# A diffusion-transformer block on one core: first scale load on ScalarE's queue, weights held until x has landed, early transposes, gate fold by copies

## The chip, the cores and the metric

The kernel runs on one NeuronCore of one Trainium2 chip. TensorE (PE) multiplies matrices, VectorE (DVE), ScalarE (ACT) and GpSimd (POOL) do elementwise work, and SyncE (SP) issues transfers; ScalarE and GpSimd can issue them as well. The transfers of all issuers are carried out by 16 DMA engines. The metric is the device time of one execution in microseconds. Before the change its median over 8 runs is 243.71 us (243.17 to 243.96).

## The reference

`x` is (2, 256, 1152) in bf16, so 512 tokens in all; `c` is (2, 1152). With D = 1152 and two heads of 576:

```python
mod = (_silu(c) @ w_mod).reshape(B, 6, 1, D)
shift_a, scale_a, gate_a, shift_m, scale_m, gate_m = [mod[:, i] for i in range(6)]
h = _layernorm(x, axis=-1) * (1 + scale_a) + shift_a
qkv = (h @ wqkv).reshape(B, N, 3, H, Dh)
attn = _softmax(jnp.einsum('bqhd,bkhd->bhqk', q, k) * Dh ** (-0.5), axis=-1)
a = jnp.einsum('bhqk,bkhd->bqhd', attn, v).reshape(B, N, D) @ wo
x = x + gate_a * a
h2 = _layernorm(x, axis=-1) * (1 + scale_m) + shift_m
m = _gelu(h2 @ w_fc1) @ w_fc2
return x + gate_m * m
```

The six modulation vectors are products of one vector per batch entry with a 1152 by 6912 matrix. The weights, some 50 MB, are read once.

## The kernel before

**Tiles and stages.** The 512 tokens are four tiles of 128 rows; tiles 0 and 1 are batch entry 0, tiles 2 and 3 batch entry 1. D is nine chunks of 128 columns. The stages follow one another on TensorE: k, q, scores, v, attention times v, the output product, the two products of the feed-forward part.

**Order of the work.** The instructions of every engine are executed in the order in which the program lists them (the loop at L819 adds an ordering from each instruction to the next of its engine). Only waits on semaphores decide when. An issued transfer needs one of a ring of eight semaphores, so a transfer issued by SyncE or ScalarE also waits for the one eight places earlier. All weights are issued by SyncE in one fixed order.

**The front.** ScalarE issues `c_sb` (L84) and `touch_x` (L86), a small read of the second batch entry. SyncE issues the four tiles of `x`, in the order 0, 1, 3, 2 (L88), and then, without a wait, the first group of `w_scale_a` (L109: chunks 0 and 1, all nine row blocks), two row blocks of `w_k` (L106), the second group of `w_scale_a`, two row blocks of `w_k`, and so on, then the last three panels of `w_k`, `w_shift_a` and `w_q`.

**Layer norm.** ScalarE sums tiles 0 and 2 (`act_stats`, L208, two passes a tile); VectorE takes tiles 1 and 3 (`stats_piece`, L195). The root of tile 2 is on ScalarE (`act_root`, `root_exp`), that of tile 3 on GpSimd. `norm1` (L235, VectorE) writes the normed tile, first columns 0 to 511, later the rest.

**Scale, transpose, modulate.** `scale_group` (L249) multiplies `w_scale_a` with the vector `sT`, 9 small products for each chunk, into a small accumulator. `scale_add` (L259) adds one. `transpose_x` (L266) turns 128x128 blocks of the normed tiles on TensorE into a bank `pt`. `modulate` multiplies a turned chunk by its scale, on VectorE (L272) or ScalarE (L274), into `hT0`. `k_step(k, ...)` (L282) adds the products of chunk k for six of the nine panels of the k matrix, in 256 columns (one batch entry) or 512 at a time; the other three panels come after (`k_panel`, L311). For chunks 0 to 3 the order is written out by hand (L360 to L397); for later chunks there is a loop (L398), in which the scales of the next two chunks and the transposes of the next chunk are placed ahead of the products of chunk k, or after the first `split` of them.

**The gate of the feed-forward part.** `gate_vector` (L463) forms `gate_m` on VectorE during the first feed-forward product: partial sums over the row blocks (L469, L471), then sums in blocks of 32 columns (L478, L479) into `folded`, 128 partitions of 72 numbers. `gate_vector_finish` (L485) adds the four groups of 32 partitions by two fp32 products with the matrix `fold` (L489), converts them (L491), writes them to DRAM (L493) and reads them back for all partitions (`broadcast_gate`, L458). It is called one panel before the end of the first product. The gate's reader is L810, the first step after each group of the second product (L804).

Of the kernel before, what the change touches and what calls it, by code (L numbers as in the profile page):

```python
# [19 lines left out]
def kernel(  # L20
# [11 lines left out]
    nc = tc.nc  # L32
    B, N, D = x.shape
# [3 lines left out]
    P = 128  # L37
    T = B * N
    NT = T // P
    TPB = N // P  # L40
    KD = D // P
    KF = F // P
# [20 lines left out]
    def aux_tile(shape, name, dt=FP32):  # L63
        return psum.tile(shape, dt, name=name, tag="aux", bufs=2)


    x_v = x.rearrange("b (p l) d -> p b l d", l=TPB)
    out_v = out.rearrange("b (p l) d -> p b l d", l=TPB)
    c_v = c.rearrange("b (k p) -> (b k) p", p=P)
    wqkv_v = wqkv.rearrange("(k p) n -> p k n", p=P)  # L70
# [11 lines left out]
    x_sb = act.tile([P, NT, D], BF16, name="x_sb", tag="x_sb")  # L82
# [2 lines left out]
    touch_x = act.tile([P, 32], BF16, name="touch_x")  # L85
    nc.scalar.dma_start(touch_x[:], x_v[:, 1, 0, 0:32])  # L86
    for t in (0, 1, 3, 2):
        nc.sync.dma_start(x_sb[:, t, :], x_v[:, t // TPB, t % TPB, :])  # L88

    zeros = const.tile([P, T], BF16, name="zeros")  # L90
    nc.vector.memset(zeros[:], 0.0)
    ident = const.tile([P, P], BF16, name="ident")
# [7 lines left out]
    SGROUPS = [(0, 2), (2, 4), (4, 6), (6, 8), (8, 9)]  # L100
    KM1 = 6
    w_scale_a = wide_tile("w_scale_a")
    w_k = wide_tile("w_k")

    def load_k(k0, k1, c0, c1):
        nc.sync.dma_start(w_k[:, k0:k1, c0:c1], wqkv_v[:, k0:k1, D + c0:D + c1])  # L106

    for k0, k1 in SGROUPS:
        nc.sync.dma_start(  # L109
            w_scale_a[:, :, k0 * P:k1 * P],  # L110
            wmod_v[:, :, S_SCALE_A * D + k0 * P:S_SCALE_A * D + k1 * P],
        )
        for a, z in [(0, 1), (1, 2)] if k0 == 0 else [(k0, k1)]:
            load_k(a, z, 0, KM1 * P)
    load_k(0, KD, KM1 * P, D)

    first_load = {}
# [12 lines left out]
    for (j0, j1), rows in zip(SHG, QROWS):  # L130
# [16 lines left out]
    hT0 = aT  # L147
# [8 lines left out]
        act_func_set_id=LN_EXP_TABLES, name=nc.get_next_instruction_name(),  # L156
        engine=mybir.EngineType.Activation,
    ))
    neg_half = const.tile([P, B], FP32, name="neg_half")
    nc.gpsimd.memset(neg_half[:], -0.5)  # L160
    early = small.tile([P, 1], FP32, name="early", tag="early", bufs=1)
# [6 lines left out]
    pwarm = acc_tile([P, T], "pwarm")  # L168
# [65 lines left out]
    def norm1(t, c0, c1):  # L234
        nc.vector.tensor_scalar(  # L235
            xns[t][:, c0:c1], x_sb[:, t, c0:c1], mv1[:, t, 0:1], rstd1[:, t:t + 1],
            op0=ALU.subtract, op1=ALU.mult,
        )


    scale_a = act.tile([P, KD, B], FP32, name="scale_a")

    def scale_group(k0, k1, tile_of=aux_tile):
        pm = tile_of([P, k1 - k0, B], "pm")
        for j in range(k0, k1):
            if j == 0:
                nc.tensor.matmul(pm[:, 0, :], ones_row[:], ones_row[:, 0:B], start=True, stop=False)
            for k in range(KD):
                nc.tensor.matmul(  # L249
                    pm[:, j - k0, :], w_scale_a[:, k, j * P:(j + 1) * P], sT[:, k, 0:B],  # L250
                    start=(k == 0 and j > 0), stop=(k == KD - 1),
                )
        return pm
# [7 lines left out]
    def transpose_x(ks, ts, pt=None, j0=0):  # L261
        if pt is None:
            pt = aux_tile([P, len(ks), len(ts) * P], "pt", BF16)
        for j, t in enumerate(ts, j0):
            for i, k in enumerate(ks):
                nc.tensor.transpose(pt[:, i, j * P:(j + 1) * P], xns[t][:, k * P:(k + 1) * P], ident[:])  # L266
        return pt

    def modulate(pt, i, k, b, j0, eng):
        dst, src, sc = hT0[:, k, b * N:(b + 1) * N], pt[:, i, j0:j0 + N], scale_a[:, k, b:b + 1]  # L270
        if eng == "d":
            nc.vector.tensor_scalar_mul(dst, src, sc)  # L272
        else:
            nc.scalar.mul(dst, src, sc)  # L274

    pk = [None] * KD

    def k_step(k, c0=0, c1=T, m0=0, m1=KM1):
        for m in range(m0, m1):
            if k == 0 and c0 == 0:  # L280
                pk[m] = acc_tile([P, T], "pk")
            nc.tensor.matmul(  # L282
                pk[m][:, c0:c1], w_k[:, k, m * P:(m + 1) * P], hT0[:, k, c0:c1],
                start=(k == 0 and c0 == 0), stop=(k == KD - 1), skip_group_check=True,
            )
# [30 lines left out]
    CUT = 4 * P  # L316
# [5 lines left out]

    def fill(n):
        for _ in range(n):
            nc.tensor.matmul(pwarm[:], zeros[:, 0:P], zeros[:], start=True, stop=True)

    def pool_eps(t):
        nc.gpsimd.tensor_scalar_add(mv1[:, t, 1:2], mv1[:, t, 1:2], LN_EPS)
# [30 lines left out]
    pool_rsqrt(3, 4)  # L359
    norm1(1, 0, CUT)  # L360
    norm1(0, 0, CUT)
    pt_a = transpose_x([0, 1], BT[0])
    act_mean_eps(2)
    act_root(2)
    root_exp(2, 3)
# [3 lines left out]
    nc.vector.tensor_copy(scale_a[:, 0:1, :], pm0[:])  # L369
    scale_add(pm1, 1, 2)  # L370
    modulate(pt_a, 1, 1, 0, 0, "d")
    norm1(2, 0, CUT)
    pt_c = aux_tile([P, 2, N], "pt", BF16)
    transpose_x([0, 1], [3], pt_c, 1)
    fill(1)
    k_step(0, 0, N)
    k_step(1, 0, N, 0, 2)
    transpose_x([0, 1], [2], pt_c, 0)
    k_step(1, 0, N, 2)
    modulate(pt_c, 0, 0, 1, 0, "d")  # L380
    modulate(pt_c, 1, 1, 1, 0, "a")
    norm1(0, CUT, D)
    norm1(1, CUT, D)
    k_step(0, N, T)
    pm = scale_group(2, 4)
    pt_b = transpose_x([2, 3], BT[0])
    scale_add(pm, 2, 4)
    modulate(pt_b, 0, 2, 0, 0, "d")
    modulate(pt_b, 1, 3, 0, 0, "a")
    norm1(2, CUT, D)  # L390
    k_step(1, N, T)
    pt_d = transpose_x([2, 3], BT[1])
    modulate(pt_d, 0, 2, 1, 0, "d")
    modulate(pt_d, 1, 3, 1, 0, "a")
    norm1(3, CUT, D)
    k_step(2, 0, N)
    k_step(2, N, T)  # L397
    for k in range(3, KD):  # L398
        split = 2 if k == 5 else 0
        k_step(k, 0, T, 0, split)  # L400
        if k in (3, 5, 7):
            k1 = min(k + 3, KD)
            scale_add(scale_group(k + 1, k1), k + 1, k1)
        if k < KD - 1:
            both(transpose_x([k + 1], range(NT)), k + 1)
        k_step(k, 0, T, split)
    for m in range(KM1):
        k_evac(m)

# [38 lines left out]

    s32 = const.tile([P, KD, B], FP32, name="s32")
    nc.vector.tensor_copy(s32[:], sT[:, :, 0:B])  # L450
    fold = const.tile([P, 32], FP32, name="fold")
    nc.vector.tensor_reduce(fold[:], ident[:].rearrange("p (q a) -> p a q", a=32), axis=AX.X, op=ALU.add)
    gates_dram = tc.dram_tile([2, B, D], BF16, name="gates_dram")

    def broadcast_gate(g):
# [7 lines left out]
    def gate_vector(g, wg):  # L463
        part = act.tile([P, B, D], FP32, name="part", tag="x_sb")
        folded = small.tile([P, B, D // 32], FP32, name="folded", tag="folded", bufs=1)
        for k in range(KD):
            for b in range(B):
                if k == 0:
                    nc.vector.tensor_scalar_mul(part[:, b, :], wg[:, k, :], s32[:, k, b:b + 1])  # L469
                else:  # L470
                    nc.vector.scalar_tensor_tensor(  # L471
                        part[:, b, :], wg[:, k, :], s32[:, k, b:b + 1], part[:, b, :],
                        op0=ALU.mult, op1=ALU.add,
                    )
        for b in range(B):
            for c in range(0, D, PW):
                blocks = work.tile([P, PW // 32, 32], FP32, name="tmp", tag="tmp", bufs=3)
                nc.vector.transpose(blocks[:].rearrange("p j r -> p (j r)"), part[:, b, c:c + PW])  # L478
                nc.vector.tensor_reduce(  # L479
                    folded[:, b, c // 32:(c + PW) // 32], blocks[:], axis=AX.X, op=ALU.add  # L480
                )

        return lambda: gate_vector_finish(g, folded)

    def gate_vector_finish(g, folded):  # L485
        rows = D // 32
        pg = aux_tile([rows, B, 32], "pg")
        for b in range(B):
            nc.tensor.matmul(pg[:, b, :], folded[:, b, :], fold[:], start=True, stop=True)  # L489
        nat = work.tile([rows, B, 32], BF16, name="nat_v", tag="nat_v", bufs=1)  # L490
        nc.vector.tensor_copy(nat[:], pg[:])  # L491
        for b in range(B):
            nc.gpsimd.dma_start(gates_dram[g, b, :].rearrange("(j r) -> j r", r=32), nat[:, b, :])  # L493
        return broadcast_gate(g)

    def gate_natural(g, wg):
# [279 lines left out]
    for m in range(MSPLIT, KF):  # L776
        pacc = acc_tile([P, T], "pacc")
        for k in range(KD):
            f1_mm(pacc[:], m, k, 0, T, k == 0)
        nc.scalar.activation(gT[:, m, :], pacc[:], ACT.Gelu_apprx_tanh)  # L780
        if m == 22:
            gate_m_finish = gate_vector(1, w_gate_m)
        if m == KF - 2:
            gate_m = gate_m_finish()
        if m == MSPLIT:
            load_f2(0)
        if m > MSPLIT and m % KD == KD - 1:
            load_f2(m // KD)
# [70 lines left out]
```

## Time and profile before

| what | value |
|---|---|
| median of 8 runs | 243.71 us |
| profiled execution: its time, its span | 243.5 us, 241.7 us |
| TensorE busy | 236.2 us, 98% of the span |
| VectorE, ScalarE, GpSimd busy | 91.4, 60.0, 28.2 us |
| moved from HBM | 50.15 MB, 212 GB/s over the span |
| granted TensorE clock | 1.00 |

The span is the time from the first to the last instruction of the profiled execution; what lies around it is 1.8 us. The page gives for each engine its busy time; the chain of work that ended last, which follows back from the last instruction what released each step; groups of instructions with their mean duration; and issues of transfers with the time from issue to landing. L numbers are lines of the kernel before. `PEld` is TensorE's loading of weights, `SPq` and `ACTq` are the issuing sides of SyncE and ScalarE. A line of the timeline has start, duration, engine, line, operation, output and input, and in brackets the idle time before it with what ended it.

### The profile page before, as it was taken

Reading aid. Unit: us, or ns where it says so; the run is one execution under the profiler, and the core shown is the slowest. Engines: PE = TensorE matmul, PEld = TensorE weight load, DVE = VectorE, ACT = ScalarE, POOL = GpSimd, SP = SyncE. Lnnn points to the kernel's source line nnn. Section 1 sums busy time; section 2 is a strip of 40 time slices with the busy share of each in tenths; the row PEclk is TensorE's granted clock in tenths of the full one; section 3 lists DMA queues with packets and bytes.
Section 4 is the critical chain, followed back from the end, with each engine's and each line's share of the span. In section 5 each row is a group of like instructions: output and inputs, shape, how many; then the busy total and the mean of one; then the engine's idle time right before and its main releaser. Section 6 shows DMA issues by size and latency. Waiting matters only on the chain.

```text
span 241.7 us, 3979 instructions
## 1 busy us (share of the span) xinstructions
PE 236.2 (98%) x1688; PEld 144.9 (60%) x1698; DVE 91.4 (38%) x193; ACT 60.0 (25%) x121; POOL 28.2 (12%) x47
## 2 busy tenths in 40 slices
PE   8899999999999999999999999999999999999994
PEld 5685444465567566888844444444665666655674
DVE  4742442319325678831002999950010000000001
ACT  6633322307215032671422333322000000000000
POOL 2300000001400324100000000001121111111111
PEclk9999999999999999999999999999999999999999
DMA  6999999996499993739999999999200000000000
GB/s 205 325 315 313 378 367 392 390 391 231 111 322 395 389 289 78 195 59 356 392 390 392 340 327 287 277 327 282 97 17 16 20 16 16 19 18 17 25 26 16
DMA packets 48926, 53.30 MB, mean 221 GB/s; under 512 B 9732, under 2 KB 36620, under 8 KB 48908
## 3 DMA queue, kind: packets, MB, share of 16 engines
q1 hardware_dynamic: 41312, 50.14, 62.2%
q10 hardware_dynamic: 7083, 1.72, 4.7%
q0 software_dynamic: 512, 1.19, 1.8%
q8 instruction: 13, 0.21, 0.4%
q14 instruction: 6, 0.04, 0.1%
HBM read 50.15 MB, written 1.19 MB: 212 GB/s over the span
## 4 chain that ended last, share of the span: by engine, by line
PE 94%; DMA 2%; ACT 1%; SPq 1%; issue 0%; DVE 0%; DVEq 0%; ACTq 0%
PE pacc L804 29%; PE pacc L748 29%; PE pacc L695 7%; PE pacc L601 7%; PE pq L523 7%; PE pk L282 5%; PE pk L311 2%; DMA x_sb<-in_x_dram 2%; PE pa L642 2%; PE ps_s L558 2%; PE pn L418 2%; ACT sink L208 1%; PE pt L266 1%; PE pm L249 1%; SPq L88 1%; PE pg L500 0%
## 5 line engine op out<-in xcount | busy, mean ns | idle before, releaser
L748 PE MATMUL pacc<-hT,w_f 128*128 128x256 bf16 (+1 forms) x427 | 70.3, 325 | 0.3
L804 PE MATMUL pacc<-w_f,gT 128*128 128x384 bf16 (+2 forms) x468 | 70.5, 314 | 0.0
L804 PEld LDWEIGHTS <-gT 128*128 128x128 bf16 x468 | 44.4, 98 | 26.2
L748 PEld LDWEIGHTS <-w_f 128*128 128x128 bf16 x432 | 42.2, 98 | 27.6
L810 DVE TENSOR_TENSOR tmp<-pacc,gate 128x384 f32<-128x384 f32 (+2 forms) x13 | 6.9, 527 | 65.6 <-PE pacc L804 56.9
L780 ACT ACTIVATE gT<-pacc 128x512 bf16<-128x512 f32 x24 | 14.3, 597 | 32.7 <-PE pacc L748 32.7
L471 DVE SCALAR_TENSOR_TENSOR part<-w_gate_m,s,part 128x1152 f32<-128x1152 bf16 x16 | 21.4, 1416 | 0.0
L812 POOL TENSOR_TENSOR o_sb<-tmp,x 128x384 bf16<-128x384 f32 (+1 forms) x12 | 11.7, 972 | 54.0 <-DVE tmp L810 54.0
L695 PE MATMUL pacc<-w_o,big 128*128 128x384 bf16 x108 | 17.9, 326 | 0.0
L523 PE MATMUL pq<-hT,w_q 128*128 128x512 bf16 x79 | 17.7, 379 | 0.1
L601 PE MATMUL pacc<-w_v,hT 128*128 128x384 bf16 x108 | 17.7, 326 | 0.0
L601 PEld LDWEIGHTS <-hT 128*128 128x128 bf16 x108 | 10.5, 98 | 7.1 <-issue 0.3
L695 PEld LDWEIGHTS <-big 128*128 128x128 bf16 x108 | 10.4, 98 | 7.2 <-issue 0.4
L523 PEld LDWEIGHTS <-w_q 128*128 128x128 bf16 x81 | 7.9, 98 | 9.4
L282 PE MATMUL pk<-big,w_k 128*128 128x256 bf16 (+1 forms) x70 | 13.1, 324 | 0.1
L701 POOL TENSOR_TENSOR x<-tmp,x_sb 128x384 f32<-128x384 f32 x8 | 7.3, 912 | 26.8 <-DMA w_scale_m<-in_w_mod_dram 14.9
L469 DVE TENSOR_SCALAR part<-w_gate_m,s 128x1152 f32<-128x1152 bf16 x2 | 1.6, 818 | 22.2 <-DMA w_gate_m<-in_w_mod_dram 22.2
L493 POOL DMA_DIRECT2D gates_dram<-nat_v x2 | 1.1, 534 | 67.7 <-DVE nat_v L491 67.7
L282 PEld LDWEIGHTS <-w_k 128*128 128x128 bf16 x72 | 6.7, 98 | 3.7 <-issue 0.3
L769 ACT ACTIVATE gT<-pacc 128x512 bf16<-128x512 f32 x12 | 6.5, 598 | 9.1 <-PE pacc L748 9.1
L175 PE MATMUL pwarm<-zeros 128*128 128x256 f32 x18 | 7.1, 565 | 1.2 <-DVE eps_t L95 1.2
L514 POOL DMA_DIRECT2D gates_dram<-nat x4 | 2.3, 584 | 49.8 <-DVE nat L511 48.8
(102 smaller groups left out, 164.8 us busy)
## 6 DMA issues: line engine op xcount, KB each, us to landing
w_f<-in_w_fc_dram SPq DMA_DIRECT2D x12, 864.0 KB, 14.3
w_f<-in_w_fc_dram SPq DMA_DIRECT2D x3, 1728.0 KB, 10.0
w_f<-in_w_fc_dram SPq DMA_DIRECT2D x2, 2592.0 KB, 17.2
w_gate_a<-in_w_mod_dram SPq DMA_DIRECT2D x3, 864.0 KB, 13.0
w_v<-in_wqkv_dram SPq DMA_DIRECT2D x3, 864.0 KB, 13.8
w_o<-in_wo_dram SPq DMA_DIRECT2D x3, 864.0 KB, 13.9
w_shift_m<-in_w_mod_dram SPq DMA_DIRECT2D x3, 864.0 KB, 8.8
w_scale_m<-in_w_mod_dram SPq DMA_DIRECT2D x3, 864.0 KB, 15.4
```

What stands on the lines that cost most here:

```text
L175: nc.tensor.matmul(dst[:, 0:T // 2], zeros32[:, 0:P], zeros32, start=True, stop=True)
L282: nc.tensor.matmul(pk[m][:, c0:c1], w_k[:, k, m * P:(m + 1) * P], hT0[:, k, c0:c1], start=(k == 0 and c0 == 0), stop=(k == KD - 1), skip_g ...
L471: nc.vector.scalar_tensor_tensor(part[:, b, :], wg[:, k, :], s32[:, k, b:b + 1], part[:, b, :], op0=ALU.mult, op1=ALU.add,)
L523: nc.tensor.matmul(pq[m][:], w_q[:, k, m * P:(m + 1) * P], hT[:, k, :], start=(k == 0), stop=(k == KD - 1), skip_group_check=True,)
L601: nc.tensor.matmul(pacc[:], hT[:, k, t * P:(t + 1) * P], w_v[:, k, pnl * PW:(pnl + 1) * PW], start=(k == 0), stop=(k == KD - 1),)
L695: nc.tensor.matmul(pacc[:], aT[:, k, t * P:(t + 1) * P], w_o[:, k, c0:c1], start=(k == 0), stop=(k == KD - 1),)
L701: (nc.gpsimd if pool_add else nc.vector).tensor_tensor(x1[:, t, c0:c1], tmp[:], x_sb[:, t, c0:c1], op=ALU.add)
L748: nc.tensor.matmul(dst, w_f1[m // KD][:, k, ml * P:(ml + 1) * P], hT[:, k, c0:c1], start=start, stop=(k == KD - 1), **kw,)
L780: nc.scalar.activation(gT[:, m, :], pacc[:], ACT.Gelu_apprx_tanh)
L804: nc.tensor.matmul(pacc[:], gT[:, kk, t * P:(t + 1) * P], w_f2[j][:, r, c0 - n * PW:c0 - n * PW + cw], start=(kk == 0), stop=(kk == KF - 1),)
L810: nc.vector.tensor_tensor(tmp[:], pacc[:], gate_m[:, b, c0:c0 + cw], op=ALU.mult)
L812: (nc.vector if last else nc.gpsimd).tensor_tensor(o_sb[:], tmp[:], x1[:, t, c0:c0 + cw], op=ALU.add)
```

## The change

1. **Loads.** The first group of `w_scale_a` (chunks 0 and 1) is issued by ScalarE, after the load of its function tables. SyncE's first load of `w_k` waits until the last tile of `x` (tile 2) has landed; all later loads of SyncE stand behind it.
2. **Transposes.** Chunks 0 to 3 of tiles 0 and 1 are turned in one go into `pt_a`, chunks 0 to 3 of tile 3 into `pt_c`; of tile 2 chunks 0 and 1 at the old place, 2 and 3 where `pt_b` was. The banks `pt_b` and `pt_d` are gone.
3. **Scale of chunks 2 and 3.** Its accumulator is a piece of `pt_a`, where chunk 0 of tile 0 stood.
4. **Modulation.** Chunks 2 and 3 of batch entry 0 are VectorE's, those of entry 1 ScalarE's. Of chunk 0 of entry 1, tile 3's half is ScalarE's and tile 2's half VectorE's.
5. **Norm.** Tile 2's first 512 columns are normed in two pieces of 256. Tile 3's rest is normed earlier.
6. **The loop.** At chunks 3 and 5 three of the six products stand ahead of the next scale group (before: none at 3, two at 5). At chunks 4 and 6 the products are done in two halves of 256 columns. The filling product `fill` has 256 columns instead of 512.
7. **Gate fold.** The products with `fold` are replaced: GpSimd copies the four groups of 32 partitions of `folded` side by side, VectorE sums, transposes and converts them, and two transfers write them to DRAM. All is done at panel 22, without a second part at panel 34.

```diff
     for t in (0, 1, 3, 2):
-        nc.sync.dma_start(x_sb[:, t, :], x_v[:, t // TPB, t % TPB, :])
+        last_x = nc.sync.dma_start(x_sb[:, t, :], x_v[:, t // TPB, t % TPB, :])
...
     def load_k(k0, k1, c0, c1):
-        nc.sync.dma_start(w_k[:, k0:k1, c0:c1], wqkv_v[:, k0:k1, D + c0:D + c1])
-
-    for k0, k1 in SGROUPS:
-        nc.sync.dma_start(
+        return nc.sync.dma_start(w_k[:, k0:k1, c0:c1], wqkv_v[:, k0:k1, D + c0:D + c1])
+
+    def load_scale(eng, k0, k1):
+        eng.dma_start(
             w_scale_a[:, :, k0 * P:k1 * P],
             wmod_v[:, :, S_SCALE_A * D + k0 * P:S_SCALE_A * D + k1 * P],
         )
+
+    for k0, k1 in SGROUPS:
+        if k0:
+            load_scale(nc.sync, k0, k1)
         for a, z in [(0, 1), (1, 2)] if k0 == 0 else [(k0, k1)]:
-            load_k(a, z, 0, KM1 * P)
+            load = load_k(a, z, 0, KM1 * P)
+            if a == 0:
+                tc.add_manual_dep(load.ins, last_x.ins.name, WAIT_FOR, reason="x first")
...
         engine=mybir.EngineType.Activation,
     ))
+    load_scale(nc.scalar, *SGROUPS[0])
...
-    def scale_group(k0, k1, tile_of=aux_tile):
-        pm = tile_of([P, k1 - k0, B], "pm")
+    def scale_group(k0, k1, tile_of=aux_tile, pm=None):
+        if pm is None:
+            pm = tile_of([P, k1 - k0, B], "pm")
...
-    def modulate(pt, i, k, b, j0, eng):
-        dst, src, sc = hT0[:, k, b * N:(b + 1) * N], pt[:, i, j0:j0 + N], scale_a[:, k, b:b + 1]
+    def modulate(pt, i, k, b, j0, eng, c0=0, c1=N):
+        dst, src, sc = hT0[:, k, b * N + c0:b * N + c1], pt[:, i, j0 + c0:j0 + c1], scale_a[:, k, b:b + 1]
...
-            nc.tensor.matmul(pwarm[:], zeros[:, 0:P], zeros[:], start=True, stop=True)
+            nc.tensor.matmul(pwarm[:, 0:N], zeros[:, 0:P], zeros[:, 0:N], start=True, stop=True)
...
-    pt_a = transpose_x([0, 1], BT[0])
+    pt_a = transpose_x([0, 1, 2, 3], BT[0])
...
-    norm1(2, 0, CUT)
-    pt_c = aux_tile([P, 2, N], "pt", BF16)
-    transpose_x([0, 1], [3], pt_c, 1)
+    norm1(2, 0, N)
+    norm1(2, N, CUT)
+    pt_c = aux_tile([P, 4, N], "pt", BF16)
+    transpose_x([0, 1, 2, 3], [3], pt_c, 1)
     fill(1)
     k_step(0, 0, N)
     k_step(1, 0, N, 0, 2)
+    modulate(pt_c, 0, 0, 1, 0, "a", P, N)
     transpose_x([0, 1], [2], pt_c, 0)
     k_step(1, 0, N, 2)
-    modulate(pt_c, 0, 0, 1, 0, "d")
+    modulate(pt_c, 0, 0, 1, 0, "d", 0, P)
     modulate(pt_c, 1, 1, 1, 0, "a")
     norm1(0, CUT, D)
     norm1(1, CUT, D)
     k_step(0, N, T)
-    pm = scale_group(2, 4)
-    pt_b = transpose_x([2, 3], BT[0])
+    pm = pt_a[:, 0, 0:4 * B].bitcast(FP32).rearrange("p (j b) -> p j b", b=B)
+    scale_group(2, 4, pm=pm)
+    for i in (2, 3):
+        nc.tensor.transpose(pt_c[:, i, 0:P], xns[2][:, i * P:(i + 1) * P], ident[:])
     scale_add(pm, 2, 4)
-    modulate(pt_b, 0, 2, 0, 0, "d")
-    modulate(pt_b, 1, 3, 0, 0, "a")
+    for b, e in enumerate("da"):
+        for i in (2, 3):
+            modulate((pt_a, pt_c)[b], i, i, b, 0, e)
     norm1(2, CUT, D)
+    norm1(3, CUT, D)
     k_step(1, N, T)
-    pt_d = transpose_x([2, 3], BT[1])
-    modulate(pt_d, 0, 2, 1, 0, "d")
-    modulate(pt_d, 1, 3, 1, 0, "a")
-    norm1(3, CUT, D)
     k_step(2, 0, N)
     k_step(2, N, T)
     for k in range(3, KD):
-        split = 2 if k == 5 else 0
+        split = 3 if k in (3, 5) else 0
...
-        k_step(k, 0, T, split)
+        for c0, c1 in ((0, N), (N, T)) if k in (4, 6) else ((0, T),):
+            k_step(k, c0, c1, split)
...
-        pg = aux_tile([rows, B, 32], "pg")
-        for b in range(B):
-            nc.tensor.matmul(pg[:, b, :], folded[:, b, :], fold[:], start=True, stop=True)
-        nat = work.tile([rows, B, 32], BF16, name="nat_v", tag="nat_v", bufs=1)
-        nc.vector.tensor_copy(nat[:], pg[:])
-        for b in range(B):
-            nc.gpsimd.dma_start(gates_dram[g, b, :].rearrange("(j r) -> j r", r=32), nat[:, b, :])
+        quads = small.tile([32, P // 32, B * rows], FP32, name="quads", tag="quads", bufs=1)
+        for a in range(P // 32):
+            nc.gpsimd.dma_start(quads[:, a, :], folded[32 * a:32 * (a + 1), :, :].rearrange("p b j -> p (b j)"))
+        total = small.tile([32, 96], FP32, name="total", tag="total", bufs=1)
+        nc.vector.memset(total[:], 0.0)
+        nc.vector.tensor_reduce(
+            total[:, 0:B * rows], quads[:].rearrange("p a c -> p c a"), axis=AX.X, op=ALU.add,
+        )
+        turned = small.tile([32, 96], FP32, name="turned", tag="turned", bufs=1)
+        nc.vector.transpose(turned[:], total[:])
+        nat = small.tile([32, 96], BF16, name="nat_v", tag="nat_v", bufs=1)
+        nc.vector.tensor_copy(nat[:], turned[:])
+        flat = gates_dram[g, :, :].rearrange("b (j r) -> (b j) r", r=32)
+        nc.gpsimd.dma_start(
+            flat[0:64, :].rearrange("(q c) r -> c q r", q=2), nat[:, 0:64].rearrange("c (q r) -> c q r", q=2),
+        )
+        nc.gpsimd.dma_start(flat[64:B * rows, :], nat[0:B * rows - 64, 64:96])
         return broadcast_gate(g)
...
         if m == 22:
-            gate_m_finish = gate_vector(1, w_gate_m)
-        if m == KF - 2:
-            gate_m = gate_m_finish()
+            gate_m = gate_vector(1, w_gate_m)
```

More of the change, by code (lines that the diff above doesn't have):

```diff
@@ L267, in transpose_x @@
         return pt
-    def modulate(pt, i, k, b, j0, eng):
-        dst, src, sc = hT0[:, k, b * N:(b + 1) * N], pt[:, i, j0:j0 + N], scale_a[:, k, b:b + 1]
+    def modulate(pt, i, k, b, j0, eng, c0=0, c1=N):
+        dst, src, sc = hT0[:, k, b * N + c0:b * N + c1], pt[:, i, j0 + c0:j0 + c1], scale_a[:, k, b:b + 1]
         if eng == "d":
-            nc.vector.tensor_scalar_mul(dst, src, sc)
-        else:
-            nc.scalar.mul(dst, src, sc)
+            return nc.vector.tensor_scalar_mul(dst, src, sc)
+        return nc.scalar.mul(dst, src, sc)
     pk = [None] * KD
@@ L450 @@
     nc.vector.tensor_copy(s32[:], sT[:, :, 0:B])
-    fold = const.tile([P, 32], FP32, name="fold")
-    nc.vector.tensor_reduce(fold[:], ident[:].rearrange("p (q a) -> p a q", a=32), axis=AX.X, op=ALU.add)
     gates_dram = tc.dram_tile([2, B, D], BF16, name="gates_dram")
@@ L481, in gate_vector @@
                 )
-        return lambda: gate_vector_finish(g, folded)
-    def gate_vector_finish(g, folded):
         rows = D // 32
-        pg = aux_tile([rows, B, 32], "pg")
-        for b in range(B):
-            nc.tensor.matmul(pg[:, b, :], folded[:, b, :], fold[:], start=True, stop=True)
-        nat = work.tile([rows, B, 32], BF16, name="nat_v", tag="nat_v", bufs=1)
-        nc.vector.tensor_copy(nat[:], pg[:])
-        for b in range(B):
-            nc.gpsimd.dma_start(gates_dram[g, b, :].rearrange("(j r) -> j r", r=32), nat[:, b, :])
+        quads = small.tile([32, P // 32, B * rows], FP32, name="quads", tag="quads", bufs=1)
[15 more added lines that the diff above has]
+        nc.gpsimd.dma_start(flat[64:B * rows, :], nat[0:B * rows - 64, 64:96])
         return broadcast_gate(g)
```

## The prediction

> **What bounds the kernel now.** I read the page's shares first, then the chain that ended last, then the front of the run.
>
> ```profile
> PE 94%; DMA 2%; ACT 1%; SPq 1%; issue 0%; DVE 0%; DVEq 0%; ACTq 0%
> ```
>
> TensorE sets the end. Only what it executes after it starts in earnest, and what makes it start late, can move the time. The chain in order of time:
>
> ```profile
> 2.10 5.38 DMA x_sb<-in_x_dram
> ...
> 7.50 1.36 ACT sink L208 x2
> ...
> 8.88 1.36 ACT sink L208 x2
> ...
> 10.64 0.21 ACT rstd L340
> ...
> 10.94 0.42 DVE xn L235
> ...
> 11.41 0.28 PE pt L266 x2
> ...
> 12.95 0.43 PE pm L249 x18
> 13.38 0.25 PE pt L266 x4
> 13.63 0.66 PE pk L282 x6
> 14.28 0.22 PE pt L266 x4
> ...
> 166.04 0.26 PE pg L489 x4
> ```
>
> (Start, length, what.) The last x tile, issued at 2.10 us, lands at 7.48. ScalarE's statistics, the root and VectorE's norm follow, and tile 2's transposes start at 11.41. From there TensorE is solid, so a later x tile is paid almost one for one. The two pt rows and the pg row are removable work.
>
> The DMA issues from 2.5 to 3.0 us (size, us from issue to landing), SyncE and ScalarE in time order at the front, and the busy time and GB/s while the first scale load moves:
>
> ```profile
> w_scale_a<-in_w_mod_dram SPq DMA_DIRECT2D x1, 576.0 KB, 6.8
> x_sb<-in_x_dram SPq DMA_DIRECT2D x1, 288.0 KB, 5.4
> ```
>
> ```profile
> 1.15 1.38 SPq L88 DMA_DIRECT2D x_sb<-in_x_dram  x3
> ...
> 1.38 0.36 ACTq L86 DMA_DIRECT2D touch_x<-in_x_dram  x1
> ...
> 1.77 1.28 ACT L155 ACT_TABLE_LOAD   x1 [1.77 <-issue]
> ...
> 2.57 0.43 SPq L109 DMA_DIRECT2D w_scale_a<-in_w_mod_dram  x1
> ```
>
> ```profile
> 6.50:7.00 0.50, 0.50 (x3) 0.41 (x2) 0.50 (x3) 0.48 (x2) 0.23 (x1) 1.00 1.08 331
> ```
>
> The scale load is issued after all x and lands at 2.57 + 6.8 = 9.4, when its products start (9.46). Its 590 KB occupy the engines for 590/331 = 1.8 us. Whatever it is put ahead of waits that long. The last view is ScalarE in the softmax stage:
>
> ```profile
> 57.59 0.49 ACT L581 ACTIVATE soft<-ps_s,negmax 128x256 f32<-128x256 f32 x1
> 57.84 1.34 ACTq L552 DMA_TRANSPOSE soft<-soft  x1
> ...
> 58.04 0.49 ACT L581 ACTIVATE soft<-ps_s,negmax 128x256 f32<-128x256 f32 x1
> ```
>
> All eight L581 instructions stand before the transpose in the program, yet it is issued while one runs and others are still to come. ScalarE's sequencer issues a DMA ahead of its unfinished computation.
>
> **What the Trainium skill says.** "DMA: Bandwidth & Descriptors", Issuing engines are not separate DMA queues: DMAs issued by ScalarE and SyncE run on the same 16 engines and interleave. The same page, Queues, rings and completion order: an engine takes the queues in turns, by packets of some descriptors, and the two issuers have a ring each. The trace agrees on sharing: from 3.50 to 4.25 us the DMA view has ScalarE's queue (q10, touch_x's small packets) beside SyncE's x. It does not show the turns.
>
> ```profile
> q10 hardware_dynamic: 144, 0.01, 12.9%
> ```
>
> "ScalarE: Activation LUTs", What ACT_TABLE_LOAD costs: about 1283 ns for the load, and it is an instruction of the engine; here 1.28 us. The page does not say that the issuing side is held meanwhile.
>
> **The change part by part.**
>
> *Work removed from TensorE.* Chunks 2-3 of tiles 0 and 1 are now transposed at 8.4 us, while TensorE waits for scales, and those of tile 3 ahead of the first k step. At 13.38 and 14.28 stood 0.25 + 0.22 = 0.47 us for eight transposes; two stay, 2 x 0.055 = 0.11: -0.36. The fold product goes: -0.26. Together -0.62 us. The shorter filler lies in a wait: 0.
>
> *Fold by copies.* VectorE is done with the blocks at 160.8 us. Four copies at 0.55 us of issue (L493's rate), some 2.6 to landing, about 1.2 of small VectorE work, two stores (1.1 + 3.6) and the broadcast (1.1 + 4.0) end near 176, against 175.2 now. Its reader L810 then has six accumulators of 5.86 us each from 168.3 before TensorE stops, at about 203. That cover hides it: 0.
>
> *Norm in two, ScalarE for a half.* Tile 2's transposes need only the first 256 columns, 0.28 instead of 0.42 us. But they write the bank from which ScalarE reads tile 3's half of chunk 0, and the built program makes them wait for that 0.37 us piece, behind the root at 10.84: about 11.2. Gain 0.1. If ScalarE's piece is slower, nothing. Chunks 2-3: after the scale products VectorE needs 0.16 + 0.35 before k step 2 starts, TensorE has 0.11 + 0.66 in between; ScalarE's 0.47 pieces have one half step more. Cover 0.2 us: 0. Scale 2-3 in the old bank waits only for a reader finished at 10.2: 0; the trace has no such shared bank, so up to 0.1 lost, nothing to gain.
>
> *Later scale groups.* Groups 4-5 are needed half a step (0.65) later than now; their landing (15.54, issue 8.14 + 7.4) leaves 0.1 to 0.3 now. This holds the k stage together if weights come late. Half-width k steps stream the same columns: 12 in 1.31 us, as 6 wide ones: 0.
>
> *First scale load on ScalarE.* It follows touch_x and the table load. If issue runs ahead of the table load, as at 57.84, it goes out at about 1.8, whereas the last x goes out at 2.06 to 2.10 (a fourth issue of 0.43 after 0.73). It then lies ahead of the x tile that sets the chain. Bounds: x not delayed (7.48) or the full 1.8 (9.3). I take 1.6, near the upper end, since touch_x too moved in the order of issue, before the later x tiles: 9.1. Behind this x tile stands more: VectorE's L215 waits for tile 2's sum (x + 1.4 = 10.5), and behind it in VectorE's order are tile 3's norm, hT0's first chunk and the scale copies, for which TensorE waits.
>
> *k loads after x.* SyncE's whole queue stops until x has landed. Then w_k 0, w_k 1 and scale 2-3 are issued 0.5 us apart. Without backlog the first x took 2.9 us to landing (0.73 to 3.63); w_k 0 is smaller: x + 2.3 to 2.8. w_k 1 adds 0.6, scale 2-3 590 KB at 310 GB/s, 1.9: it lands at x + 5.0 to 5.5. Now it lands at 4.66 + 7.8 = 12.46 with x at 7.48, so x + 5.0. With x on time this costs 0 to 0.5, since the removed backlog pays for the wait.
>
> *Sum.* The scale 2-3 products start at x + 5.47 now (12.95). After: computation path x + 5.37, load path x + 5.0 to 5.5, so about x + 5.4. With x at 9.1: 14.5, +1.5; less 0.62: +0.9 us. Later weight loads shift with TensorE and keep their margin (the k panel: landed about 24.2, needed 25.7). The span becomes 242.6, this execution 244.4; the median of the runs stands 0.2 above the profiled 243.5, so **244.6**.
>
> **Rivals.**
>
> *Issue behind x.* The table load holds the issue to 3.05, or the engines serve x first: x stays at 7.48. Then -0.1 + 0.1 - 0.62: about -0.6, **243.1**. This ends on the other side; it decides where the scale load delays x by less than 0.1 to 0.2 us, since below that the gain passes 0.5. For it: the table load stands between. Against: 57.84.
>
> *Turns.* The engines alternate, as the skill says, and x loses only part: 0.4 to 0.9. Then +0.6 - 0.62 = 0: **243.8**. For it: the skill; against: touch_x came in one piece.
>
> *x alone is quicker.* Nothing competes, and x lands by 6.8. ScalarE is free from 7.23, so its path gains 0.25, and the loads start 0.6 earlier: -0.4 - 0.62 = -1.0: **242.7**. Against: the x loads already lead their queue, and DMA's share is near 1 there either way.
>
> **How the numbers follow.** Scale ahead of x 0.51; turns 0.22; behind x 0.17; x quicker 0.10. The likeliest gives 244.6, own range 244.1 to 245.3 (x 8.6 to 9.5, load path to +0.5). All cases: 242.8 to 245.4. A measurement can tell about 0.2%, 0.49 us, from no change. Faster: x quicker 0.10 and most of behind x (0.14) = 0.24; same: most of turns, a rest of behind x and of the first = 0.22; slower 0.54.
>
> **What would show it.** The issue of the scale load at 1.8, not 3.05; landing of tile 2 of x at 9 or later, ScalarE idle before L208's second pair by over 1.5 us; SyncE's w_k issue right after that; scale 2-3 products at 14.5 with DMA as releaser at the front. No pg product near 166 and six fewer transposes in the chain. I am wrong if x lands by 7.6, or if TensorE waits for loads after 15 us.

## The result

| | before | changed |
|---|---|---|
| median of the runs | 243.61 us (243.08 to 245.02) | 247.09 us (245.63 to 248.38) |
| profiled execution: time, span | 243.5, 241.7 us | 245.63, 243.8 us |
| last tile of x landed | 7.47 us | 8.79 us |
| scale 2-3 landed | 12.5 us | 15.36 us |
| products of scale 2-3 start | 12.95 us | 15.41 us |
| q stage starts | 32.55 us | 35.01 us |
| second feed-forward product starts | 168.34 us | 170.44 us |

The changed kernel is slower: ratio 1.0134, 95% interval [1.0117, 1.0152], or +3.3 us. The forecast had the sign and the place, and 2.5 us too little. The profiled execution is the quickest of its kernel's runs, so its trace explains 2.1 us of the loss; what the others add is found further down. (247.09 is the median of eleven times; the list of runs has a twelfth, 246.08, with which it would be 246.95.)

The shares of the chain that ended last, in the page of the changed kernel, and then that chain in order of time (start, length, what):

```profile
PE 85%; DMA 7%; SPq 5%; issue 1%; DVE 0%; DVEq 0%
```

```profile
2.10 6.70 DMA x_sb<-in_x_dram
8.79 0.02 issue
8.81 0.33 SPq L106
...
9.66 0.43 SPq L109
...
21.42 10.70 DMA w_shift_a<-in_w_mod_dram
32.11 0.04 issue
32.16 0.81 PE pn L428 x36
...
35.01 5.18 PE pq L538 x24
...
167.26 3.19 PE pacc L763 x14
170.44 70.30 PE pacc L817 x468
```

Before, TensorE held 94% of this chain and transfers 2%. Now the chain runs from the late x tile into SyncE's queue, then into a weight load, and reaches TensorE only at 32 us. The end is quiet: no fold product stands between the two feed-forward products, and the 468 products of the second take 70.30 us in both kernels.

The timeline of the changed kernel at the front (start, duration, engine and line, what, and in brackets the idle time before it with what ended it):

```profile
1.78 1.28 ACT L161 ACT_TABLE_LOAD   x1 [1.78 <-issue]
1.81 0.41 ACTq L109 DMA_DIRECT2D w_scale_a<-in_w_mod_dram  x1
...
8.82 1.25 ACT L215 ACTIVATE sink<-x_sb 128x1152 f32<-128x1152 bf16 x1 [1.44 <-DMA x_sb<-in_x_dram]
...
15.41 0.60 PE L257 MATMUL pt<-sT,w_scale_a 128*128 128x2 bf16 x18 [1.20 <-DMA w_scale_a<-in_w_mod_dram]
```

ScalarE's issuing side sent the scale load at 1.81 us, while the table load that stands ahead of it in the program was running, and 0.3 us before SyncE's last x tile went out at 2.10. ScalarE then waits for x, and TensorE waits at 15.41 for scale 2-3. Two loads stop TensorE, as the list of its waits over the first 35 us says (total, times, longest):

```profile
PE pt L257 <- DMA w_scale_a<-in_w_mod_dram: 1.2, 1, 1.2
...
PEld L428 <- DMA w_shift_a<-in_w_mod_dram: 0.6, 1, 0.6
```

What the DMA engines did meanwhile is in the busy times by stretch. The last two columns are their busy share and GB/s. First the kernel before, then the changed one:

```profile
8.00:11.00 3.00, 2.39 (x35) 1.64 (x34) 1.77 (x9) 2.69 (x6) 1.30 (x4) 1.00 1.12 325
11.00:14.00 3.00, 2.90 (x42) 2.30 (x41) 1.89 (x7) 0.47 (x1) 0.00 (x0) 1.00 1.13 319
```

```profile
8.00:11.00 3.00, 1.75 (x29) 1.21 (x28) 2.48 (x8) 2.15 (x3) 1.33 (x4) 1.00 0.48 137
11.00:14.00 3.00, 2.79 (x34) 2.07 (x30) 2.38 (x9) 1.77 (x6) 0.00 (x0) 1.00 0.96 237
```

The engines run dry. From 8 to 14 us they move 3 x (137 + 237) = 1,120 KB instead of 3 x (325 + 319) = 1,930 KB. At 322 GB/s the missing 810 KB are 2.5 us of transfer, about the 2.46 us by which the products of scale 2-3 are late. The match is rough: between 5 and 8 us another 150 KB are missing (250 against 300 GB/s), and a landing also depends on how evenly the 16 engines finish, as is shown further down.

### The profile page after: what moved, and what is told of

The parts are those of the page before. It is cut to its first block, busy times and chain, and to the rows that moved or that the text cites. A ratio compares the mean times of both kernels' runs of the same rounds, so it can differ in the third digit from the quotient of the medians.

```text
span 243.8 us, 4006 instructions
## 1 busy us (share of the span) xinstructions
PE 236.2 (97%) x1695; PEld 146.1 (60%) x1706; DVE 92.4 (38%) x196; ACT 60.1 (25%) x122; POOL 30.3 (12%) x51
## 4 chain that ended last, share of the span: by engine, by line
PE 85%; DMA 7%; SPq 5%; issue 1%; DVE 0%; DVEq 0%
PE pacc L817 29%; PE pacc L763 29%; PE pacc L710 7%; PE pacc L616 7%; PE pq L538 7%; DMA w_shift_a<-in_w_mod_dram 4%; SPq L106 4%; DMA x_sb<-in_x_dram 3%; PE pa L657 2%; PE ps_s L573 2%; PE pn L428 2%; PE pk L318 1%; SPq L109 1%; SPq L88 1%; PE pg L515 0%
## 5 line engine op out<-in xcount | busy, mean ns | idle before, releaser
L616 PEld LDWEIGHTS <-hT 128*128 128x128 bf16 x108 | 10.5, 98 | 7.1 <-issue 0.3
L494 POOL DMA_DIRECT2D quads<-folded x4 | 2.0, 508 | 62.2 <-DVE total L496 62.2
L289 PEld LDWEIGHTS <-w_k 128*128 128x128 bf16 x84 | 7.9, 98 | 2.5 <-issue 0.2
## 6 DMA issues: line engine op xcount, KB each, us to landing
w_scale_m<-in_w_mod_dram SPq DMA_DIRECT2D x3, 864.0 KB, 14.5
```

What stands on the lines that cost most here:

```text
L289: nc.tensor.matmul(pk[m][:, c0:c1], w_k[:, k, m * P:(m + 1) * P], hT0[:, k, c0:c1], start=(k == 0 and c0 == 0), stop=(k == KD - 1), skip_g ...
L616: nc.tensor.matmul(pacc[:], hT[:, k, t * P:(t + 1) * P], w_v[:, k, pnl * PW:(pnl + 1) * PW], start=(k == 0), stop=(k == KD - 1),)
```

## The experiments

Two causes were in question: the scale load that overtakes x ("late x"), and SyncE's queue, which stops until x has landed ("the hold"). The forecast's theory was that late x costs nearly all and the hold at most 0.5 us; the rival that the hold alone, by emptying the DMA engines, costs as much or more.

**e1: the change with its loads as before.**

```diff
-        if k0:
-            load_scale(nc.sync, k0, k1)
+        load_scale(nc.sync, k0, k1)
...
-            if a == 0:
-                tc.add_manual_dep(load.ins, last_x.ins.name, WAIT_FOR, reason="x first")
...
-    load_scale(nc.scalar, *SGROUPS[0])
```

> The changed kernel, but with all loads where they were before: first scale load by SyncE behind x, no hold of the k loads. Theory L (the loads alone cost; the rest removes 0.36 + 0.26 us of TensorE work and 0 to 0.1 of waiting): x lands at 7.5, scale 2-3 at 12.5, the time is 243.0, 0.5 to 0.7 us under the kernel before. Rival R (part of the loss is in the rest: shared bank, later scale groups, halves of k steps): 244 or more, with a wait of TensorE on VectorE or ScalarE between 11 and 25 us.

Measured: 242.92 us, 0.9974 [0.9962, 0.9986], as the theory had it. x landed at 7.49, scale 2-3 at 12.45, as before. All of the loss is in the loads; the rest of the change gains 0.3% or 0.6 us (interval 0.3 to 0.9), the size of the work removed.

**e2: the loads alone.** The kernel before, with part 1 of the change (loads) and nothing else.

```diff
-    for k0, k1 in SGROUPS:
-        nc.sync.dma_start(
...
+    def load_scale(eng, k0, k1):
+        eng.dma_start(
...
+    for k0, k1 in SGROUPS:
+        if k0:
+            load_scale(nc.sync, k0, k1)
...
+            if a == 0:
+                tc.add_manual_dep(load.ins, last_x.ins.name, WAIT_FOR, reason="x first")
...
+    load_scale(nc.scalar, *SGROUPS[0])
```

> The kernel before with only the change of the loads: first scale load by ScalarE behind the table load, k loads held until x has landed. Theory L: the whole loss and none of the gain, so 0.6 us above the changed kernel, about 247.7; with none of its scale groups needed later, up to 0.5 more. Rival R: clearly under the changed kernel, 246 or less.

Measured: 246.87 us, 1.0132 [1.0116, 1.0148]. x landed at 8.19 and scale 2-3 at 14.98, 6.8 us behind it. The loads alone cost as much as the whole change, 247.09, and not the 0.6 us more that was expected (247.7). So the 0.6 us that e1 gains is not to be seen, within these intervals, while TensorE waits for loads. That fits work taken out ahead of a wait, which only lengthens the wait; it is not shown alone, since in e2's profile x and scale 2-3 also land 0.6 and 0.4 us sooner than in the changed kernel.

**e3: late x alone, and e4: the hold alone.** e3 takes the wait out of the changed kernel; e4 keeps the wait and gives the first scale load back to SyncE, behind x.

```diff
-            if a == 0:
-                tc.add_manual_dep(load.ins, last_x.ins.name, WAIT_FOR, reason="x first")
```

```diff
-        if k0:
-            load_scale(nc.sync, k0, k1)
+        load_scale(nc.sync, k0, k1)
...
-    load_scale(nc.scalar, *SGROUPS[0])
```

> The changed kernel without the hold: k loads go out behind x at once, the first scale load stays with ScalarE. If the place of the scale load ahead of the last x tiles is the cause: x lands at 8.5 to 9.4 as in the changed kernel, scale 2-3 at about 12.5 to 13, the time is set by x + 5.4 and the removed work, 244.0 to 244.8. If the hold is the whole cause: 243.0. If the hold is without effect: 247.

> The changed kernel with the hold, but the first scale load by SyncE behind x as before. x lands at 7.5, scale 2-3 at x + 6.6 (as measured in the changed kernel, not x + 5.0 to 5.5 as I had it) = 14.1, its products 1.1 later than before; less 0.6 of removed work: 244.0 to 245.0. If the restart of the stream costs nothing (x + 5.2): 243.2. If the hold is the whole cause: 247.

Measured: e3 245.40 us, 1.0075 [1.0052, 1.0098]; e4 245.42 us, 1.0076 [1.0051, 1.0101]. Against e1 each cause costs 2.5 us by the medians of four runs, and each is there without the other. Both medians lie over what was expected (244.0 to 244.8, and 244.0 to 245.0). Two of the four runs of each have a lower clock, of which more below; at full clock the costs are 1.8 and 1.7 us. So the rival was right about the hold: alone it costs as much as late x. In e3 the last x tile lands at 2.10 + 7.62 = 9.72 us. The scale load itself comes later there too (11.18 us, 9.41 before), but the chain still runs through x. In e4 x lands in time (7.44), and yet scale 2-3 comes 7.15 us behind it; the chain of waits of e4 and its timeline:

```profile
2.10 5.34 DMA x_sb<-in_x_dram
...
8.32 6.29 DMA w_scale_a<-in_w_mod_dram
```

```profile
14.65 0.60 PE L255 MATMUL pt<-sT,w_scale_a 128*128 128x2 bf16 x18 [1.79 <-DMA w_scale_a<-in_w_mod_dram]
```

**e5: the order of issue without a second queue.** e1, but SyncE itself issues the first scale load ahead of the last x tile.

```diff
     for t in (0, 1, 3, 2):
+        if t == 2:
+            load_scale(nc.sync, 0, 2)
```

> As the first experiment (all loads by SyncE, no hold), but the first scale load is issued by SyncE ahead of the last x tile instead of behind it. If the order of issue is what delays x, whatever the queue: the last x tile lands 1.5 to 2 later than 7.5, at 9.0 to 9.7, scale 2-3 stays at about 12.5, the time is as without the hold on ScalarE's queue, 244.5 to 245.5. If it took the second queue: x lands by 8.2 (only the issue 0.45 later), 243.0 to 243.6.

Measured: 244.91 us, 1.005 [1.0033, 1.0066]. The x tile of e5 in the chain of waits:

```profile
2.58 6.70 DMA x_sb<-in_x_dram
```

It lands at 9.28, against 7.49 in e1. ScalarE's queue is not needed for the delay: 590 KB ahead of x in the order of issue are enough, 1.8 us as the forecast had it.

**e6 and e7: a shorter and a longer hold.** e4, with the k loads waiting for tile 1 of x (landed at 4.40 us), or for the first scale load (9.14 us).

```diff
-                tc.add_manual_dep(load.ins, last_x.ins.name, WAIT_FOR, reason="x first")
+                tc.add_manual_dep(load.ins, x_loads[1].ins.name, WAIT_FOR, reason="x first")
```

```diff
-                tc.add_manual_dep(load.ins, last_x.ins.name, WAIT_FOR, reason="x first")
+                tc.add_manual_dep(load.ins, scale_load.ins.name, WAIT_FOR, reason="x first")
```

> As the experiment with the hold alone, but the k loads wait for x tile 1 (landed at 4.4 to 4.7) and not for the last. The first k load goes out 1.5 later than unheld, while x and the scale load still keep the DMA engines busy to about 7.3. If the idle gap of the DMA engines costs: no gap, scale 2-3 at 12.5 to 12.7, 242.9 to 243.3. If any hold costs by its own, or costs in proportion to its length (a third of the 2.5 us): 243.7 or more.

> As the experiment with the hold alone, but the k loads wait for the first scale load (landed at 9.2 to 9.8), not for x (7.5): the gap is 1.7 to 2.3 longer. If the gap costs: k load 0 lands at 11.5 to 12.2 and holds the first k step, scale 2-3 at 16.3 to 16.8, 247.2 to 247.8. If the cost is a fixed one of a restart: 245.4 as before.

Measured: e6 242.79 us, 0.9965 [0.9952, 0.9978]; e7 247.91 us, 1.0177 [1.0154, 1.02]. Busy times by stretch of e6, of e4 and of e7:

```profile
8.00:11.00 3.00, 2.40 (x40) 2.00 (x40) 2.02 (x9) 2.82 (x7) 1.41 (x4) 1.00 1.14 339
11.00:14.00 3.00, 2.95 (x42) 2.40 (x41) 2.15 (x9) 0.99 (x3) 0.00 (x0) 1.00 1.13 321
```

```profile
8.00:11.00 3.00, 2.88 (x43) 2.12 (x41) 2.09 (x9) 2.84 (x7) 1.34 (x4) 1.00 0.75 207
11.00:14.00 3.00, 1.69 (x14) 1.00 (x12) 1.51 (x5) 0.55 (x2) 0.00 (x0) 1.00 1.08 326
```

```profile
8.00:11.00 3.00, 1.61 (x32) 1.27 (x32) 2.14 (x10) 2.84 (x7) 1.40 (x4) 1.00 0.29 74
11.00:14.00 3.00, 2.42 (x14) 1.88 (x15) 0.97 (x4) 0.21 (x2) 0.00 (x0) 0.65 0.96 258
```

With the wait still in the queue but over while x is still moving, the stream has no gap (339 and 321 GB/s), scale 2-3 lands at 12.32, and nothing is lost. Held 1.7 us longer than in e4, the stream falls to 74 GB/s, scale 2-3 lands at 16.94, and the time is 2.5 us over e4. What costs is the gap in the stream of loads, not the wait as such. A fixed cost of a restart (245.4 for e7) is excluded.

**e8: the fold alone.** The kernel before, with part 7 of the change (gate fold by copies).

```diff
-    fold = const.tile([P, 32], FP32, name="fold")
...
-            nc.tensor.matmul(pg[:, b, :], folded[:, b, :], fold[:], start=True, stop=True)
...
+            nc.gpsimd.dma_start(quads[:, a, :], folded[32 * a:32 * (a + 1), :, :].rearrange("p b j -> p (b j)"))
```

> The kernel before with only the gate fold by copies. The 0.26 us of fp32 products near 166 go, the copies stay hidden behind the first groups of the second product: 243.4, 0.26 under the kernel before. If the copies come late and stop TensorE: over 243.7, with a wait of the second product after 200 us.

Measured: 243.28 us against 243.54 in the same session, 0.9986 [0.9977, 0.9994]. The gain is that of the product, 0.26 us (interval 0.15 to 0.56), and the copies are hidden: the 468 products of the second feed-forward product take 70.31 us without a break.

**e9: ScalarE's load behind x.** The changed kernel, but ScalarE issues its load when tile 0 of x has landed (issue at 3.50 us).

```diff
-    load_scale(nc.scalar, *SGROUPS[0])
+    late = load_scale(nc.scalar, *SGROUPS[0])
+    tc.add_manual_dep(late.ins, first_x.ins.name, WAIT_FOR, reason="behind x")
```

> The changed kernel, but ScalarE issues the first scale load only when x tile 0 has landed (3.7), behind the issue of all x. The queue is the changed kernel's, the order of issue that of before. If the engines serve by order of issue: x lands at 7.4 to 7.6 and the time is that of the hold alone, 245.0 to 245.8. If they take turns between the queues: x lands at 8.0 or later, 246 or more.

Measured: 243.93 us, 1.0011 [1.0002, 1.0021]; neither forecast was met. The chain of waits:

```profile
2.10 4.81 DMA x_sb<-in_x_dram
...
7.78 5.56 DMA w_scale_a<-in_w_mod_dram
```

Issued behind x, ScalarE's load does not delay it: x lands at 6.92, and between 7.08 and 7.50 in the six profiles in which SyncE issues all x first and this load behind it. So the hold ends sooner too, the stream thins less (241 GB/s from 8 to 11 us, against 207 in e4), and scale 2-3 lands at 13.34 instead of 14.60.

Its transfer took 5.56 us here and 6.29 in e4. The difference is in the slowest engines. A load is spread over the 16 DMA engines, and the trace has the end of each engine's part. For scale 2-3, in us, "release" being the end of the wait:

| kernel | release | w_k 1 landed | half of the parts | 14 of 16 | last | half and last, from the release |
|---|---|---|---|---|---|---|
| before | no wait | 10.49 | 11.18 | 12.15 | 12.50 | x + 3.71, x + 5.03 |
| e6 | 4.40 | 10.35 | 11.06 | 12.00 | 12.32 | x + 3.71, x + 4.97 |
| changed | 8.79 | 11.75 | 13.95 | 15.04 | 15.36 | 5.16, 6.57 |
| e2 | 8.19 | 11.21 | 13.34 | 14.83 | 14.98 | 5.15, 6.79 |
| e4 | 7.45 | 10.52 | 12.53 | 12.72 | 14.60 | 5.08, 7.15 |
| e7 | 9.14 | 12.19 | 14.26 | 14.89 | 16.94 | 5.12, 7.80 |
| e9 | 6.92 | 9.98 | 12.19 | 12.52 | 13.34 | 5.27, 6.42 |

Half of the parts are there 5.1 to 5.3 us after the release in every kernel whose stream had a gap. The last one follows 1.1 to 2.7 us later (0.8 to 1.3 in the seven profiles without a gap), and TensorE waits for it; in e4 two engines alone make up 1.9 us. Which engines lag, and why, stays open; these are single profiles.

**e10 and e11: filling TensorE's idle time.** The profiles of e2, e3, e5 and e7 have a stretch of 3.4 us (e7 two) in which the granted clock of TensorE is 0.50 (the eighth number). That of e5:

```profile
12.00:13.00 1.00, 1.00 (x6) 0.42 (x4) 0.25 (x1) 0.79 (x4) 0.00 (x0) 0.52 1.15 316
13.00:14.00 1.00, 0.90 (x7) 0.66 (x7) 0.69 (x4) 0.02 (x1) 0.00 (x0) 0.50 1.20 299
14.00:15.00 1.00, 1.00 (x6) 0.74 (x5) 0.65 (x2) 0.45 (x1) 0.00 (x0) 0.50 1.08 332
```

e10 is e5 with three more filling products, in the stretch from 9.8 to 11.2 us where TensorE stood idle. e11 is the changed kernel with three more of them ahead of the first transposes.

```diff
     pm0, pm1 = [scale_group(k, k + 1, acc_tile) for k in range(2)]
+    warm(3, pwarm)
```

```diff
-    warm(7, pwarm)
+    warm(10, pwarm)
```

> This is the kernel of e5 (SyncE issues scale 0-1 ahead of the last x tile, no hold) with three more 128x256 fp32 matmuls into the unused accumulator behind the first scale products, where TensorE stood idle from 9.8 to 11.2 us in e5 and the clock then read 0.50 from 12 to 15.2 us. Theory (the idle TensorE is what the clock answered; the x tile's delay costs the rest): the clock stays at 1.00 from 12 to 15 us, ten k products take 1.3 us again instead of 2.1, and the time is about 0.8 us under e5, some 244.1 us. Rival (the clock falls for another reason, or what it slows is hidden): the time stays at 244.9, within 0.3.

> This is the changed kernel with ten warming matmuls instead of seven ahead of the first transposes, so that TensorE is busy until about 9.7 us instead of 8.7, where it then waited 1.25 us for the normalised x. The idle stretch from 14.2 to 15.4 us stays. Theory (an idle stretch brings the clock down in those executions whose mean clock is 0.991 to 0.993): if the first stretch is the one that matters, the mean clocks are 0.998 or more and the median falls by 0.5 to 1.0 us, to 246.1 to 246.6; if it is the later one, the split between 0.992 and 1.0 stays and so does 247.1. Rival (the clock has no part in the loss): the time stays at 247.1 whatever the clocks read.

Measured: e10 244.79 us, 1.0029 [1.0016, 1.0042]; e11 246.26 us, 1.0099 [1.0074, 1.0123]. The same stretches of e10:

```profile
12.00:13.00 1.00, 0.86 (x8) 0.52 (x6) 0.22 (x2) 0.88 (x5) 0.00 (x0) 1.00 1.14 328
13.00:14.00 1.00, 0.61 (x6) 0.52 (x7) 0.80 (x4) 0.15 (x1) 0.00 (x0) 1.00 1.21 300
14.00:15.00 1.00, 0.99 (x17) 0.80 (x15) 0.78 (x3) 0.47 (x1) 0.00 (x0) 1.00 1.09 329
```

The clock stays at 1.00, and all fifteen runs of e10 have a mean of 0.998 or more, where two of four of e5 had 0.993. So it is the idle time that the clock answers. What that is worth is not settled: e5 was 1.2 us above the kernel before of its session (243.74) and e10 0.8 above that of its own (244.00). The intervals overlap, and a gain of anything from nothing to 1 us fits, so neither the 0.8 of the theory nor the rival's none is excluded.

In e11 three of six runs still have a mean of 0.991 to 0.993, so the stretch that was filled is not the only one that brings the clock down. Of the two outcomes expected neither came whole: the split stayed, and yet the median is 0.8 us lower (in another session). The runs of each kernel by their mean clock:

| kernel | clock 0.998 or more | lower clock (0.986 to 0.993) |
|---|---|---|
| changed | 245.63, 246.03, 246.08, 246.66, 248.38 | 246.11, 246.81, 247.09, 247.37, 247.40, 247.48, 247.81 |
| e2 | 246.14, 246.68 | 247.06, 247.23 |
| e3 | 244.63, 244.78 | 246.01, 246.16 |
| e4 | 244.61, 244.68 | 246.16, 246.19 |
| e5 | 244.55, 244.80 | 245.02, 245.49 |
| e7 | 247.73 | 247.24, 248.08, 248.49 |
| e11 | 245.70, 246.08, 246.15 | 246.38, 246.96, 247.09 |

By their medians the runs with the lower clock are longer by 0.6 to 1.5 us in six rows, in the changed kernel by 1.3 (246.08 and 247.37). The clock is not all of the scatter: the changed kernel's 248.38 was at full clock, and in e7 the fastest run is one with the lower clock. Of e1, e6, e8 and e9 no run is below 0.998; of the kernel before two of 20 are, in the session of e10.

The profiles tell more. In all 13 the clock changes only at the ends of stretches of 3.41 us or whole multiples of it, and where these stretches lie differs from one execution to the next. At the front of the run, five of them are followed by one at 0.50. Busy times in the stretch ahead of the fall in e2, e3 and e5 (e7 has 1.93 and 1.92 us of PE), and then in the two least busy ones that no fall follows, in e4 and in e11 (the number after the length is PE's busy time):

```profile
11.71:15.12 3.41, 1.69 (x16) 1.09 (x16) 1.42 (x4) 0.47 (x1) 0.00 (x0) 1.00 1.02 291
9.98:13.39 3.41, 1.86 (x31) 1.47 (x31) 1.54 (x7) 3.21 (x7) 0.57 (x2) 1.00 1.15 322
8.62:12.03 3.41, 1.95 (x37) 1.69 (x37) 1.24 (x6) 2.69 (x4) 0.84 (x3) 1.00 1.11 330
```

```profile
10.65:14.06 3.41, 2.04 (x17) 1.20 (x15) 1.60 (x5) 0.90 (x3) 0.00 (x0) 1.00 1.08 322
13.59:17.00 3.41, 2.11 (x35) 1.69 (x34) 1.28 (x6) 0.85 (x3) 0.00 (x0) 1.00 1.06 309
```

At the front a fall came after 1.69 to 1.95 us of work, 49 to 57% of the stretch, and none after 2.04 us, 60%, or more. Wherever a stretch of this length is laid over the front of e1, e6, e8, e9 or e10, TensorE is busy for at least 64% of it, and none of their 65 runs fell. That would explain why the same kernel falls in one execution and not in the next: it depends on how its idle time lies in the stretches. With one profile of each kernel this is not shown. The boundary is not exact. Around the last products of e2 and e10 stretches of 57 and 55% brought no fall, and the kernel before, whose profile has no front stretch under 79%, had its two runs nonetheless.

**The sum.** At full clock e1 has 242.9 us, late x (e3) adds 1.8 and the hold (e4) 1.7; both together (246.1) add 3.2, so they overlap by 0.3. Seven of twelve runs with the lower clock bring the median from 246.1 to 247.0 or 247.1. Few runs stand behind each of these figures.

## Why the prediction was right and wrong

**First scale load on ScalarE: right.** The issue was at 1.81 us and x landed at 8.79, where 9.1 was taken and 9.3 was the upper bound. The rival *Issue behind x* is excluded by the issue at 1.81 and by e5. *Turns* would have had x at 7.9 to 8.4: e2, with the same loads, is there (8.19), the changed kernel and e3 (9.72) are beyond it. The Trainium skill ("DMA: Bandwidth & Descriptors", Queues, rings and completion order) lets the engines alternate between the issuers' rings. Here the delay in two rings varied between profiled executions from 0.7 to 2.2 us, around the 1.8 that one ring showed (e5), and was gone when the load was issued behind x (e9): the order of issue decides, and some taking of turns is not excluded. *x alone is quicker* shows only in e9, with x at 6.92, and there the hold took the gain back.

**k loads after x: the step that failed.** Its first half holds: w_k 0 landed at x + 2.42, within 2.3 to 2.8, and w_k 1 0.54 later, where 0.6 was taken. What failed is the last term, "scale 2-3 590 KB at 310 GB/s, 1.9": scale 2-3 landed 3.61 us after w_k 1, at x + 6.57 instead of x + 5.0 to 5.5, and in e4 at x + 7.15. The term takes the 16 engines at their mean rate. Half of them were indeed done at x + 5.16; a load has landed when the last one is done, and that was 1.41 us later (2.07 in e4).

So the comparison with "now", x + 5.0, was uneven: that landing was measured, with 1.3 us between half and last in it, while the forecast's had none. Like for like, half of the parts were done at x + 3.71 before and at x + 5.16 now. These 1.4 to 1.5 us are what the removed backlog was worth, and it did not "pay for the wait". With x on time the hold was priced at 0 to 0.5 us and costs 1.7 (e4 against e1, at full clock). The rate, too, came back unevenly. Stretches of the changed kernel:

```profile
10.50:11.00 0.50, 0.50 (x19) 0.49 (x18) 0.32 (x1) 0.50 (x1) 0.44 (x2) 1.00 0.99 307
11.50:12.00 0.50, 0.50 (x7) 0.44 (x6) 0.36 (x2) 0.38 (x3) 0.00 (x0) 1.00 0.54 110
```

307 GB/s were reached 1.7 us after the first issue; then the stream thinned once more, although scale 2-3 had been issued at 9.66 and the next load at 10.13. Why, no run shows.

**Later weight loads: wrong.** They were to "shift with TensorE and keep their margin". w_shift_a was issued at 21.42 instead of 18.27, 3.15 us later, for a TensorE that was 2.46 us later, and TensorE's weight loads waited 0.6 us for it. Of TensorE's own time this is some 0.3: from the products of scale 2-3 to those of w_shift_a it takes 16.75 us, and 16.47 in e1. From the products of scale 2-3 to the q stage both kernels take 19.60 us, so the 0.36 us of removed transposes came to nothing here.

**Work removed: right in size.** e8 has the 0.26 us of the fold, e1 about 0.6 for all. In the changed kernel only the part at the end counts: the delay falls from 2.46 us at the q stage to 2.10 at the second product.

**Fold by copies: right in the result, by luck in the sum.** The gate arrived at 177.97 us, not 176, in a stage that ran 2.1 us late, and TensorE's 468 products ran through. Inside, two errors cancel: from the first copy's issue to the last landing it took 7.1 us (163.78 to 170.88), not 2.2 + 2.6, and the stores and the broadcast 5.6 us (172.33 to 177.97), not 9.8.

**Sum.** 14.5 us was forecast for the products of scale 2-3, 15.41 measured: 0.9. With the 0.36 us that was not saved this makes 1.3, close to the 1.2 us between the span forecast (242.6) and that of the profile (243.8). The other 1.3 us of the miss is the median's height above the profiled execution, 1.5 instead of 0.2. Of it 1.0 goes with the clock, as far as twelve runs tell; the forecast had no term for it. The Trainium skill has one ("TensorE: Matmul & The Clock Gate", Part 1: The HAM clock gate (the "warmup" mystery)): half rate after an idle window of about 3.4 us, which runs free, so that runs of one kernel differ. The stretches of 3.41 us and the differing runs agree with that. But a whole idle window is not needed here: TensorE was busy for 49 to 57% of the stretches ahead of the falls, and the longest single gap at the front of e5 was 1.46 us.

## What to carry to other kernels

A wait put into a queue of loads costs nothing while transfers in flight cover it (e6), and costs once the stream runs dry: e4 put off the first k load from 3.05 to 7.46 us and lost 1.7 us at full clock, and the 1.7 us more of e7 cost another 2.5 by the medians. Watch GB/s by stretch and the last engine's part, not the landing of the load that was meant to gain. A load moved to another engine's queue takes its place by the time of its issue, which can lie ahead of computation that stands before it in the program; it delays what is issued after it, here by 0.7 to 2.2 us for 1.8 us of bytes. Both e1 (242.92 us) and e6 (242.79 us) keep the gain of the rest of the change and beat both kernels: x leads, and the loads behind it never pause.

## What was not expected of the hardware

- TensorE's clock fell to 0.50 for 3.41 us after stretches of 3.41 us in which it was busy for 1.69 to 1.95 us, with single gaps of only 1 to 1.5 us in e5, in some runs of a kernel and not in others. Such runs were 0.6 to 1.5 us longer in six of seven kernels. With the gap filled it stayed at 1.00 in fifteen runs out of fifteen (e10).
- After a gap the DMA engines came back in two steps. In the changed kernel (issue at 8.81) they moved 307 GB/s from 10.5 to 11.0 us, 110 from 11.5 to 12.0, and over 330 only from 15; in e4 (issue at 7.46) 312 from 9.5 to 10.0, 145 from 10.0 to 10.5, and 309 from 11.0.
- In e4 the parts of one transfer of 590 KB, scale 2-3, were complete between 12.18 and 14.60 us, according to the engine that carried them, 14 of 16 by 12.72: the slowest sets the landing.
